# Block-sparse attention and a spatial-gating MLP: the MLP's projections interleaved, and the transposed q, k pairs split into their tiles by DMAs instead of VectorE copies

## The chip, the cores and the metric

The kernel runs on one core of one Trainium2 chip. The metric is device time in microseconds (us), lower is better. A core has five engines that run their own instruction streams and wait for one another by semaphores: TensorE (PE in the profile, with its weight loads as PEld), VectorE (DVE), ScalarE (ACT), GpSimd (POOL) and SyncE (SP), which here only issues DMAs. The DMAs are carried out by 16 DMA engines.

## The reference, cut to what matters

Attention over 4 batches of 8 heads, 768 positions, head size 64, under a block mask (blocks of 32: neighbours, first and last row and column, and three sampled blocks per row), followed by a gated MLP along the sequence:

```python
scores = scale * np.matmul(q, k.transpose(0, 1, 3, 2))        # B=4, H=8, S=768, D=64
scores = np.where(mask, scores, -1000000000.0)
attn = np.exp(scores - max) ; attn = attn / (sum + 1e-09)
x = np.matmul(attn, v)                                        # heads side by side: B, S, 512
h = np.maximum(x @ w_in, 0.0)                                 # 512 -> 1024
u, v = h[..., :512], h[..., 512:]
v_n = (v - mu) / np.sqrt(var + 1e-06)                         # over the 512 features
v_s = np.einsum('ts,bsd->btd', w_spatial, v_n) + b_spatial[None, :, None]
out = (u * v_s) @ w_out                                       # 512 -> 512
```

## The kernel before

**Staging.** Heads are handled in pairs; there are 16 pairs (p = 0 to 15), four to a batch. Loads of q, k, v (`load`, in float32, on SyncE's queue) run three pairs ahead. GpSimd casts them to bfloat16 (`prepare`: `nat_k`, `nat_q`, and `vv`). The scores need q and k with the head dimension on partitions, so each pair is transposed: for the first six pairs by TensorE (`tr_head`, `tr_pair`), for pairs 6 to 15 by a DMA transpose on SyncE (`tr_dma`), which puts both heads of the pair into one tile `tt_k` or `tt_q` of 128 partitions, the first head in partitions 0 to 63, the second in 64 to 127.

**The mask tiles.** The mask enters the scores as extra rows of the product: the tiles `qt[0..3]` and `kt[0..3]` have 64 rows of data and 24 rows that encode the block mask. Head j uses tiles j % 4. So the transposed pair must be split: rows 0 to 63 of `tt` go to rows 0 to 63 of one tile, rows 64 to 127 to rows 0 to 63 of the next. `split_pair` does that.

**The main loop** has 12 slots per pair, six per head. In a slot TensorE makes the scores of one chunk of 128 keys (`qk_exp`, two matmuls of 384 columns), ScalarE takes their exponential into `a_all`, TensorE pops some matmuls of the MLP of the batch before (from the deque `moe_q`), and multiplies one chunk of the head of seven slots earlier by its values (`av`, six matmuls; VectorE normalizes a finished head in `norm`). Slot numbers place the rest: `split_pair` of the next pair's k in slot 5 and q in slot 9, loads and `prepare` in slot 7, the DMA transposes of the pair after next (`tr_dma`) in slot 10. The program is emitted in this order and each engine runs its own part of it strictly in order, SyncE's queue included.

**The MLP** of one batch is a list of 108 matmuls of 512 columns (`moe_units`): 24 for v (six chunks of positions, four matmuls each), 24 for u, 36 for the spatial product and 24 for the output. They are spread over the 48 slots that follow slot 8 of the first pair of the next batch (52 for the third batch), about 2.25 per slot. After the four matmuls of a v chunk `v_post` takes the Relu (VectorE in the loop, ScalarE for the last batch), then the statistics on VectorE (`bn_stats`, `bn_aggr`); after every third chunk GpSimd makes the reciprocal deviations of three (`std`, `rstd`). After the four matmuls of a u chunk `u_post` takes the Relu of u on ScalarE and normalizes the v chunk of the same number (`vn`) on VectorE. The spatial product reads all six `vn`; its result becomes `gn` on VectorE and is transposed to `gt` by a DMA on SyncE, which the output matmuls read. The MLP of the last batch runs after the loop, with nothing beside it, with its gn transposed on TensorE.

**The start.** TensorE runs matmuls of zeros (`keep_warm`) between the first transposes, so that its clock rises.

Of the kernel before, what the change touches and what calls it, by code (L numbers as in the profile page):

```python
# [10 lines left out]
FP32 = mybir.dt.float32  # L11
BF16 = mybir.dt.bfloat16
I32 = mybir.dt.int32
AF = mybir.ActivationFunctionType
ALU = mybir.AluOpType
# [11 lines left out]
def kernel(  # L27
# [16 lines left out]
    nc = tc.nc  # L44

    B, H, S, D = q.shape
# [3 lines left out]
    NCH = S // 128  # L50
    HALF = S // 2
    DM = H * D
    DFF = moe_w_in.shape[1]
    DH = DFF // 2
    NDM = DM // 128
    NDH = DH // 128
    NG = H // 2
    NP = B * NG
# [5 lines left out]
    work = ctx.enter_context(tc.tile_pool(name="work", bufs=1))  # L64
# [5 lines left out]
    w_in_t = const.tile([128, NDM, DFF], BF16)  # L70
# [4 lines left out]
    mhalf = const.tile([128, NCH], FP32)  # L75

    qt = [const.tile([KR, S], BF16, name=f"qt{s}") for s in range(4)]
    kt = [const.tile([KR, S], BF16, name=f"kt{s}") for s in range(4)]
# [99 lines left out]
    def keep_warm(n, cols):  # L178
        for _ in range(n):
            nc.tensor.matmul(out=wps[:, 0:cols], lhsT=warm[:, 0:128], rhs=warm[:, 0:cols],  # L180
                             start=True, stop=True)
# [26 lines left out]
    for r in range(NR):  # L208
        nc.vector.scalar_tensor_tensor(out=allowed, in0=colidx,
                                       scalar=samp_f[:, 2 * r:2 * r + 1], in1=allowed,  # L210
                                       op0=ALU.is_equal, op1=ALU.max)
    bm = const.tile([NB, NB], BF16)
    nc.vector.tensor_scalar(out=bm, in0=allowed, scalar1=1.0, scalar2=-MASK_NEG,
                            op0=ALU.subtract, op1=ALU.mult)
# [3 lines left out]
                         func=AF.Copy)  # L218
# [6 lines left out]
    def tr_head(h, nm, copy):  # L225
        ps = psum.tile([128, S], BF16, tag="moe", bufs=2)
        for c in range(NCH):
            nc.tensor.transpose(out=ps[0:D, c * 128:(c + 1) * 128], in_=nat[nm, 0][:, c, h],  # L228
                                identity=ident)
        copy((qt if nm == "q" else kt)[h][0:D, :], ps[0:D, :])  # L230
# [15 lines left out]

    tr_head(0, "k", dve_copy)
    nc.vector.tensor_copy(out=kt[0][D:KR, :], in_=ind)
    keep_warm(2, 128)
    mq = psum.tile([128, 1024], FP32, tag="sc", bufs=2, name="mq")  # L250
    for hf in range(2):
        nc.tensor.matmul(out=mq[0:NB, hf * 512:hf * 512 + HALF], lhsT=bm,
                         rhs=ind[:, hf * HALF:(hf + 1) * HALF], start=True, stop=True)
    act_copy(qt[0][D:KR, :].rearrange("p (b c) -> p b c", b=2),
             mq[0:NB].rearrange("p (b c) -> p b c", b=2)[:, :, 0:HALF])
    tr_head(0, "q", dve_copy)
    keep_warm(6, 128)

    def mask_rows(sl):
        nc.vector.tensor_copy(out=kt[sl][D:KR, :], in_=kt[0][D:KR, :])  # L260
# [7 lines left out]
    tt = {}  # L268
# [3 lines left out]
        nc.sync.dma_start_transpose(out=tt[nm, p],  # L272
                                    in_=nat.pop((nm, p)).rearrange("p c h d -> p (c h d)"))

    def split_pair(p, nm):
        src = tt.pop((nm, p)).rearrange("x c n -> x (c n)")
        for h in range(2):
            nc.vector.tensor_copy(out=(qt if nm == "q" else kt)[(2 * p + h) % 4][0:D, :],  # L278
                                  in_=src[h * D:(h + 1) * D, :])


# [79 lines left out]
    def moe_units(b):  # L361
        last = b == B - 1
        units = []
        un = work.tile([128, NCH, DH], BF16, tag="un", bufs=2)
        vsb = work.tile([128, NCH, DH], BF16, tag="vsb", bufs=2)
        vn = work.tile([128, NCH, DH], BF16, tag="vn", bufs=2)
        gn = work.tile([128, NCH, DH], BF16, tag="gn", bufs=2)
        gt = work.tile([128, NCH, NDH, 128], BF16, tag="gt", bufs=2)
        mv = work.tile([128, NCH, 2], FP32, tag="mv", bufs=2)
        std = work.tile([128, NCH], FP32, tag="std", bufs=2)  # L370
        rstd = work.tile([128, NCH], FP32, tag="rstd", bufs=2)

        def xt(g):
            return xt_ref[b * NG + g]

        def add(n, operands, post):


            box = []

            def step(i):
                if i == 0:
                    box.append(moe_ps(last))
                lhs, rhs = operands(i)
                nc.tensor.matmul(out=box[0], lhsT=lhs, rhs=rhs,  # L385
                                 start=(i == 0), stop=(i == n - 1))
                if i == n - 1:
                    post(box[0])
            units.extend((lambda i=i: step(i)) for i in range(n))

        for tcc in range(NCH):
            def v_post(ps, tcc=tcc):
                if last:
                    nc.scalar.activation(out=vsb[:, tcc, :], in_=ps, func=AF.Relu)  # L394
                else:
                    nc.vector.tensor_scalar(out=vsb[:, tcc, :], in0=ps, scalar1=0.0,  # L396
                                            scalar2=None, op0=ALU.max)
                stats = work.tile([128, 6], FP32, tag="stats", bufs=2)
                nc.vector.bn_stats(out=stats, in_=vsb[:, tcc, :])  # L399
                nc.vector.bn_aggr(out=mv[:, tcc, :], in_=stats)  # L400
                if tcc % 3 == 2:
                    cs = slice(tcc - 2, tcc + 1)
                    nc.gpsimd.tensor_scalar(out=std[:, cs], in0=mv[:, cs, 1], scalar1=1e-6,  # L403
                                            scalar2=None, op0=ALU.add)
                    nc.gpsimd.tensor_tensor(out=rstd[:, cs], in0=std[:, cs],
                                            in1=mhalf[:, cs], op=ALU.pow)
            add(NDM, lambda g, tcc=tcc: (xt(g)[:, tcc * 128:(tcc + 1) * 128],
                                         w_in_t[:, g, DH:DFF]), v_post)

        for tcc in range(NCH):  # L410
            def u_post(ps, tcc=tcc):
                nc.scalar.activation(out=un[:, tcc, :], in_=ps, func=AF.Relu)  # L412
                nc.vector.tensor_scalar(out=vn[:, tcc, :], in0=vsb[:, tcc, :],
                                        scalar1=mv[:, tcc, 0:1],
                                        scalar2=rstd[:, tcc:tcc + 1],
                                        op0=ALU.subtract, op1=ALU.mult)
            add(NDM, lambda g, tcc=tcc: (xt(g)[:, tcc * 128:(tcc + 1) * 128],
                                         w_in_t[:, g, 0:DH]), u_post)

        def g_tr(tcc):  # L420
            ps = psum.tile([128, S], BF16, tag="moe", bufs=2, name="ps_g")
            for dhc in range(NDH):
                nc.tensor.transpose(out=ps[:, dhc * 128:(dhc + 1) * 128],  # L423
                                    in_=gn[:, tcc, dhc * 128:(dhc + 1) * 128],
                                    identity=ident)
            act_copy(gt[:, tcc].rearrange("p c n -> p (c n)"), ps[:, 0:DH])

        for tcc in range(NCH):
            def s_post(ps, tcc=tcc):
                nc.vector.scalar_tensor_tensor(out=gn[:, tcc, :], in0=ps,  # L430
                                               scalar=b_col[:, tcc:tcc + 1],
                                               in1=un[:, tcc, :], op0=ALU.add, op1=ALU.mult)
                if not last:
                    nc.sync.dma_start_transpose(out=gt[:, tcc], in_=gn[:, tcc, :])
                elif tcc > 0:
                    g_tr(tcc - 1)
            add(NCH, lambda sc, tcc=tcc: (w_spt[:, sc, tcc * 128:(tcc + 1) * 128],
                                          vn[:, sc, :]), s_post)

        for tcc in range(NCH):  # L440
            def o_post(ps, tcc=tcc):
                osb = work.tile([128, DM], FP32, tag="osb", bufs=6)
                if last and tcc == NCH - 1:
                    nc.scalar.activation(out=osb[:, 0:DM // 2], in_=ps[:, 0:DM // 2],
                                         func=AF.Copy)
                    nc.vector.tensor_copy(out=osb[:, DM // 2:DM], in_=ps[:, DM // 2:DM])
                elif tcc % 2 == 0:
                    nc.scalar.activation(out=osb, in_=ps, func=AF.Copy)
                else:
                    nc.vector.tensor_copy(out=osb, in_=ps)  # L450
                nc.sync.dma_start(
                    out=out[b].rearrange("(p c) d -> c p d", c=NCH)[tcc], in_=osb)
            if last and tcc == 1:
                units.append(lambda: g_tr(NCH - 1))
            add(NDH, lambda dhc, tcc=tcc: (gt[:, tcc, dhc, :], w_out_t[:, dhc, :]), o_post)
        return units
# [7 lines left out]
    for p in range(NP + 1):  # L464
        for s in range(12):
            g = 12 * p + s
# [15 lines left out]
            if p <= NG:  # L482
                first = 0 if p else 6
                if first <= s < first + 3:
                    tr_pair(p + 1, "k", s - first)
                elif first + 3 <= s < first + 6:
                    tr_pair(p + 1, "q", s - first - 3)
            elif p + 1 < NP and s in (5, 9):
                split_pair(p + 1, "k" if s == 5 else "q")
            if s == 10 and NG + 1 < p + 2 < NP:  # L490
                tr_dma(p + 2, "k")
                tr_dma(p + 2, "q")
# [68 lines left out]
```

The softmax here doesn't subtract the row's maximum and nothing guards it: scores larger than these inputs give would overflow.

## Time and profile before

| what | value |
|---|---|
| time, median of three runs | 224.88 us (224.37 to 226.83) |
| span of the profiled run | 224.2 us |
| TensorE busy | 214.1 us, 95% |
| VectorE busy | 128.1 us, 57% |
| ScalarE busy | 177.5 us, 79% |
| GpSimd busy | 64.4 us, 29% |
| copies that split k (`kt<-tt_k`, 20) | 9.5 us on VectorE |
| copies that split q (`qt<-tt_q`, 20) | 7.0 us on VectorE |
| statistics of v (`stats`, 24) | 16.7 us on VectorE |
| first exponential | 8.9 us after the span's start |
| last exponential | starts at 187.4 us |

Busy shares are averages over the start, the loop without an MLP (up to about 50 us), the loop with one (to about 190 us) and the tail (to the end); these have different limits. In the profile's lines a group is named by its source line, its engine, and the tiles written and read; "SPq" is SyncE's DMA queue, and the length shown there is that of issuing the transfer, not of the transfer.

### The profile page before, as it was taken

The numbers are of one execution on the slowest core, as the hardware profiler recorded it, in microseconds if no ns is written. First come the engines' busy times: TensorE is split into PE (matmuls) and PEld (weight loads), VectorE is DVE, ScalarE is ACT, GpSimd is POOL, SyncE is SP. The second block draws the span as 40 slices with busy tenths as digits, with TensorE's granted clock in tenths as the row PEclk, the third lists the DMA queues.
The fourth block names the chain that finished last, engine by engine and source line by source line (L and its number), as shares of the span: only waits on it lengthen the run. The fifth ranks groups of instructions, "written<-read, shape, count | busy, mean of one in ns | idle before, by whom it ended". The sixth has DMA issues, their size and how long they took to land.

```text
span 224.2 us, 5285 instructions
## 1 busy us (share of the span) xinstructions
PE 214.1 (95%) x2117; PEld 130.7 (58%) x2148; DVE 128.1 (57%) x282; ACT 177.5 (79%) x246; POOL 64.4 (29%) x88
## 2 busy tenths in 40 slices
PE   7999999999999999999899999999999999999993
PEld 3567777775555655665556666566556665544551
DVE  5465554556984445268983454359993433584531
ACT  5599999998789888887699888888899885266351
POOL 5435751429950701210650301210620000012000
PEclk9999999999999999999999999999999999999999
DMA  6679989996799796999756286989050224620016
GB/s 210 212 228 392 389 287 339 330 168 73 204 299 155 234 133 183 195 298 275 236 105 213 48 108 195 218 290 272 4 105 6 55 50 82 213 96 0 0 50 235
DMA packets 56093, 40.27 MB, mean 180 GB/s; under 512 B 39300, under 2 KB 51588, under 8 KB 56068
## 3 DMA queue, kind: packets, MB, share of 16 engines
q1 hardware_dynamic: 55780, 39.53, 67.3%
q10 hardware_dynamic: 288, 0.39, 0.5%
q8 instruction: 17, 0.28, 0.5%
q14 instruction: 8, 0.07, 0.1%
HBM read 24.38 MB, written 6.29 MB: 137 GB/s over the span
## 4 chain that ended last, share of the span: by engine, by line
PE 69%; DVE 14%; ACT 13%; issue 2%; DMA 2%; SPq 0%
PE ps_moe L385 24%; PE ps L289 19%; ACT a_all L293 12%; PE ps_av L305 10%; PE ps_t L385 7%; DVE vsb L396 4%; DVE stats L399 4%; PE ps_sc L385 4%; PE wps L180 2%; DVE kt L278 2%; DMA st_q<-in_q_dram 2%; DVE xn L319 2%; PE ps L228 1%; DVE mv L400 1%; PE ps_g L423 1%
## 5 line engine op out<-in xcount | busy, mean ns | idle before, releaser
L293 ACT ACTIVATE a_all<-ps 128x768 bf16<-128x768 f32 x192 | 149.9, 816 | 21.8 <-PE ps L289 13.7
L289 PE MATMUL ps<-qt,kt 88*128 88x384 bf16 x384 | 94.6, 327 | 1.3 <-DVE qt L244 0.5
L305 PEld LDWEIGHTS <-a_all 128*128 128x128 bf16 x1152 | 60.4, 97 | 39.3 <-issue 3.4
L305 PE MATMUL ps_av<-vv,a_all 128*128 128x65 bf16 x1152 | 67.8, 194 | 0.2
L385 PE MATMUL ps_moe<-w_in_t,xt 128*128 128x512 bf16 x130 | 39.6, 378 | 2.5 <-DVE vsb L396 1.8
L289 PEld LDWEIGHTS <-kt 88*128 88x128 bf16 x384 | 28.4, 98 | 4.0 <-issue 1.2
L385 PE MATMUL ps_moe<-vn,w_spt 128*128 128x512 bf16 x99 | 30.0, 378 | 0.5
L112 POOL CAST vv<-st_v 128x768 bf16<-128x768 f32 x16 | 13.5, 844 | 54.3 <-PE ps_av L305 51.1
L385 PEld LDWEIGHTS <-xt 128*128 128x128 bf16 x192 | 18.6, 97 | 16.1 <-issue 0.3
L430 DVE SCALAR_TENSOR_TENSOR gn<-ps_moe,b_col,un 128x512 bf16<-128x512 f32 x18 | 13.5, 749 | 18.9 <-PE ps_moe L385 15.6
L318 DVE RECIPROCAL rc<-ps_av 128x6 f32<-128x6 f32 x32 | 6.1, 190 | 26.1 <-PE ps_av L305 26.0
L403 POOL TENSOR_SCALAR std<-mv 128x3 f32<-128x3 f32 x8 | 2.0, 244 | 63.2 <-DVE mv L400 63.1
L385 PEld LDWEIGHTS <-w_spt 128*128 128x128 bf16 x144 | 13.7, 97 | 10.8
L385 PE MATMUL ps_moe<-w_out_t,gt 128*128 128x512 bf16 x66 | 19.1, 378 | 0.5 <-DVE gn L430 0.3
L319 DVE TENSOR_TENSOR xn<-ps_av,rc 128x384 bf16<-128x384 f32 x32 | 17.8, 558 | 1.1
L109 POOL CAST nat_k<-st_k 128x768 bf16<-128x768 f32 x15 | 12.4, 828 | 18.5 <-DMA st_k<-in_k_dram 13.9
L399 DVE BATCH_NORM_STATS2 stats<-vsb 128x6 f32<-128x512 bf16 x24 | 16.7, 694 | 1.5 <-ACT vsb L394 0.8
L396 DVE TENSOR_SCALAR vsb<-ps_moe 128x512 bf16<-128x512 f32 x18 | 12.3, 682 | 3.0 <-PE ps_moe L385 3.0
L109 POOL CAST nat_q<-st_q 128x768 bf16<-128x768 f32 x15 | 12.9, 859 | 0.0
L385 PEld LDWEIGHTS <-gt 128*128 128x128 bf16 x96 | 8.8, 97 | 6.9
L278 DVE COPY kt<-tt_k 64x768 bf16<-64x768 bf16 x20 | 9.5, 476 | 4.3 <-DMA tt_k<-nat_k 4.1
L412 ACT ACTIVATE un<-ps_moe 128x512 bf16<-128x512 f32 x18 | 11.0, 609 | 0.0
(80 smaller groups left out, 172.4 us busy)
## 6 DMA issues: line engine op xcount, KB each, us to landing
st_v<-in_v_dram SPq DMA_DIRECT2D x16, 384.0 KB, 5.5
out_dram<-osb SPq DMA_DIRECT2D x24, 256.0 KB, 2.5
st_q<-in_q_dram SPq DMA_DIRECT2D x15, 384.0 KB, 3.9
st_k<-in_k_dram SPq DMA_DIRECT2D x15, 384.0 KB, 4.9
wst<-in_moe_w_spatial_dram SPq DMA_DIRECT2D x3, 768.0 KB, 8.7
wst<-in_moe_w_in_dram SPq DMA_DIRECT2D x4, 512.0 KB, 9.2
wst<-in_moe_w_out_dram SPq DMA_DIRECT2D x2, 512.0 KB, 6.7
st_k<-in_k_dram ACTq DMA_DIRECT2D x2, 192.0 KB, 2.9
```

Source lines behind the costliest of these rows:

```text
L109: eng.tensor_copy(out=dst, in_=src)
L112: nc.gpsimd.tensor_copy(out=vv[p % 3][:, :, :, 0:D], in_=st.pop(("v", p)).rearrange("p h (c d) -> p h c d", d=D))
L278: nc.vector.tensor_copy(out=(qt if nm == "q" else kt)[(2 * p + h) % 4][0:D, :], in_=src[h * D:(h + 1) * D, :])
L289: nc.tensor.matmul(out=ps[:, hf * 512:hf * 512 + HALF], lhsT=kt[j % 4][:, ci * 128:(ci + 1) * 128], rhs=qt[j % 4][:, hf * HALF:(hf + 1) * ...
L293: nc.scalar.activation(out=a_ref[j][:, ci, :].rearrange("p (b c) -> p b c", b=2), in_=ps.rearrange("p (b c) -> p b c", b=2)[:, :, 0:HALF], ...
L305: nc.tensor.matmul(out=av_ref[j][:, qc, :], lhsT=a_ref[j][:, ci, qc * 128:(qc + 1) * 128], rhs=vv[p % 3][:, h, ci, :], start=(ci == 0), st ...
L319: nc.vector.tensor_tensor(out=xn_ref[p][:, :, h, :], in0=ps[:, :, 0:D], in1=rc.to_broadcast([128, NCH, D]), op=ALU.mult)
L385: nc.tensor.matmul(out=box[0], lhsT=lhs, rhs=rhs, start=(i == 0), stop=(i == n - 1))
L396: nc.vector.tensor_scalar(out=vsb[:, tcc, :], in0=ps, scalar1=0.0, scalar2=None, op0=ALU.max)
L399: nc.vector.bn_stats(out=stats, in_=vsb[:, tcc, :])
L412: nc.scalar.activation(out=un[:, tcc, :], in_=ps, func=AF.Relu)
L430: nc.vector.scalar_tensor_tensor(out=gn[:, tcc, :], in0=ps, scalar=b_col[:, tcc:tcc + 1], in1=un[:, tcc, :], op0=ALU.add, op1=ALU.mult)
```

## The change

It does two things, with some change at the start.

First, v and u chunks of the MLP are interleaved: v0, v1, v2, u0, v3, u1, v4, u2, v5, u3, u4, u5, where before came six v and then six u. The normalization of v chunk i moves from the u chunk i to the u chunk i + 1, the last two both to the last. This is to spread VectorE's statistics over a longer time and to give the reciprocal deviations time to come.

Second, `split_pair` issues plain DMAs from SBUF to SBUF on SyncE's queue, all four of a pair in slot 4, where VectorE made four copies in slots 5 and 9. This is to free VectorE of them. Ten pairs are split in this way, so 40 copies become 40 DMAs of 64 rows of 1536 bytes.

Third, `keep_warm` runs six more matmuls of 128 columns before the first scores.

```diff
-    keep_warm(2, 128)
+    keep_warm(4, 128)
     mq = psum.tile([128, 1024], FP32, tag="sc", bufs=2, name="mq")
...
+    keep_warm(2, 128)
     tr_head(0, "q", dve_copy)
-    keep_warm(6, 128)
+    keep_warm(8, 128)
...
-    def split_pair(p, nm):
-        src = tt.pop((nm, p)).rearrange("x c n -> x (c n)")
-        for h in range(2):
-            nc.vector.tensor_copy(out=(qt if nm == "q" else kt)[(2 * p + h) % 4][0:D, :],
+    def split_pair(p):
+        for nm in "kq":
+            src = tt.pop((nm, p)).rearrange("x c n -> x (c n)")
+            for h in range(2):
+                nc.sync.dma_start(out=(qt if nm == "q" else kt)[(2 * p + h) % 4][0:D, :],
                                   in_=src[h * D:(h + 1) * D, :])
...
-        for tcc in range(NCH):
-            def u_post(ps, tcc=tcc):
-                nc.scalar.activation(out=un[:, tcc, :], in_=ps, func=AF.Relu)
-                nc.vector.tensor_scalar(out=vn[:, tcc, :], in0=vsb[:, tcc, :],
-                                        scalar1=mv[:, tcc, 0:1],
-                                        scalar2=rstd[:, tcc:tcc + 1],
-                                        op0=ALU.subtract, op1=ALU.mult)
...
+        def u_post(tcc, ps):
+            nc.scalar.activation(out=un[:, tcc, :], in_=ps, func=AF.Relu)
+            if tcc > 0:
+                normalize(tcc - 1)
+            if tcc == NCH - 1:
+                normalize(tcc)
...
+        for i in range(NCH + 2):
+            if i < NCH:
+                in_proj(i, slice(DH, DFF), v_post)
+            if i >= 2:
+                in_proj(i - 2, slice(0, DH), u_post)
...
-            elif p + 1 < NP and s in (5, 9):
-                split_pair(p + 1, "k" if s == 5 else "q")
+            elif p + 1 < NP and s == 4:
+                split_pair(p + 1)
```

More of the change, by code (lines that the diff above doesn't have):

```diff
@@ L389, in add @@
             units.extend((lambda i=i: step(i)) for i in range(n))
-        for tcc in range(NCH):
[L392 to L408, printed above, removed]
@@ L410, in moe_units, with v_post @@
-        for tcc in range(NCH):
-            def u_post(ps, tcc=tcc):
-                nc.scalar.activation(out=un[:, tcc, :], in_=ps, func=AF.Relu)
-                nc.vector.tensor_scalar(out=vn[:, tcc, :], in0=vsb[:, tcc, :],
-                                        scalar1=mv[:, tcc, 0:1],
-                                        scalar2=rstd[:, tcc:tcc + 1],
-                                        op0=ALU.subtract, op1=ALU.mult)
-            add(NDM, lambda g, tcc=tcc: (xt(g)[:, tcc * 128:(tcc + 1) * 128],
-                                         w_in_t[:, g, 0:DH]), u_post)
+        def v_post(tcc, ps):
+            if last:
+                nc.scalar.activation(out=vsb[:, tcc, :], in_=ps, func=AF.Relu)
+            else:
+                nc.vector.tensor_scalar(out=vsb[:, tcc, :], in0=ps, scalar1=0.0,
+                                        scalar2=None, op0=ALU.max)
+            stats = work.tile([128, 6], FP32, tag="stats", bufs=2)
+            nc.vector.bn_stats(out=stats, in_=vsb[:, tcc, :])
+            nc.vector.bn_aggr(out=mv[:, tcc, :], in_=stats)
+            if tcc % 3 == 2:
+                cs = slice(tcc - 2, tcc + 1)
+                nc.gpsimd.tensor_scalar(out=std[:, cs], in0=mv[:, cs, 1], scalar1=1e-6,
+                                        scalar2=None, op0=ALU.add)
+                nc.gpsimd.tensor_tensor(out=rstd[:, cs], in0=std[:, cs],
+                                        in1=mhalf[:, cs], op=ALU.pow)
@@ new lines, in normalize @@
+        def normalize(tcc):
+            nc.vector.tensor_scalar(out=vn[:, tcc, :], in0=vsb[:, tcc, :],
+                                    scalar1=mv[:, tcc, 0:1],
+                                    scalar2=rstd[:, tcc:tcc + 1],
+                                    op0=ALU.subtract, op1=ALU.mult)
+        def u_post(tcc, ps):
[4 more added lines that the diff above has]
+                normalize(tcc)
@@ L420, in g_tr, with in_proj @@
+        def in_proj(tcc, cols, post):
+            add(NDM, lambda g: (xt(g)[:, tcc * 128:(tcc + 1) * 128], w_in_t[:, g, cols]),
+                lambda ps: post(tcc, ps))
+        for i in range(NCH + 2):
[3 more added lines that the diff above has]
+                in_proj(i - 2, slice(0, DH), u_post)
         def g_tr(tcc):
```

## The prediction

> **What bounds the kernel now.** I read the page first: TensorE is busy 95% of the span, and the chain that ended last is 69% TensorE, 14% VectorE, 13% ScalarE. An average over stages decides nothing, so I cut the span into the iterations of the outer loop (one head pair each, from the first exponential of a pair to that of the next, taken from the ScalarE timeline) and asked for busy times in each. The six that matter, with columns us of the stretch, then busy us of TensorE, weight loads, VectorE, ScalarE, GpSimd:
>
> ```profile
> 54.06:66.71 12.65, 12.06 (x122) 7.23 (x124) 12.00 (x26) 10.59 (x14) 10.00 (x11) 1.00 0.98 234
> 66.71:78.78 12.07, 11.96 (x122) 7.23 (x124) 5.40 (x14) 11.11 (x18) 5.17 (x6) 1.00 0.92 198
> ...
> 103.34:116.51 13.17, 12.11 (x123) 7.23 (x124) 12.52 (x26) 10.59 (x14) 5.74 (x9) 1.00 0.74 208
> 116.51:128.58 12.07, 11.96 (x123) 7.24 (x124) 5.36 (x14) 11.10 (x18) 3.13 (x4) 1.00 0.47 131
> ...
> 152.92:165.14 12.22, 11.68 (x121) 7.04 (x122) 11.46 (x26) 10.17 (x13) 4.58 (x7) 1.00 0.46 119
> 165.14:176.78 11.64, 11.47 (x120) 7.04 (x122) 5.21 (x15) 11.21 (x17) 0.38 (x1) 1.00 0.27 52
> ```
>
> See the pairs of lines: each holds a v stage, then the u stage after it. In the u stage TensorE is busy 11.96 of 12.07 us: that is its pace. In the v stage VectorE is busy 12.00 of 12.65 us, and the iteration is longer by 0.58, 1.10 and 0.58 us (12.65, 13.17, 12.22 less 12.07, 12.07, 11.64). That is 2.26 us, the whole of what VectorE costs in the loop. The chain in order of time agrees: in these stretches it leaves TensorE for VectorE, the k copies among its links.
>
> ```profile
> 104.23 0.71 DVE stats L399
> ...
> 108.87 0.76 DVE kt L278
> 109.65 0.89 DVE kt L278
> 110.53 0.61 DVE vsb L396
> ```
>
> Third, the timeline of the SyncE queue in the spatial stage of the second batch (start, length):
>
> ```profile
> 137.87 1.20 SPq L434 DMA_TRANSPOSE gt<-gn  x1
> 139.16 1.36 SPq L342 DMA_TRANSPOSE xt<-xn  x1
> 140.61 1.25 SPq L272 DMA_TRANSPOSE tt_k<-nat_k  x1
> 141.96 1.24 SPq L272 DMA_TRANSPOSE tt_q<-nat_q  x1
> 143.29 1.22 SPq L434 DMA_TRANSPOSE gt<-gn  x1
> 144.60 2.91 SPq L451 DMA_DIRECT2D out_dram<-osb  x4
> ```
>
> These follow one another with some 0.1 us between: from 127.06 to 152 us the queue, not what it waits for, sets when a transfer is issued. The last gt there has its gn ready at 139.51 and is issued only at 143.29.
>
> **What the Trainium skill says.** "DMA: Bandwidth & Descriptors", section "Two DMAs through the same engine are not ordered": a DMA that reads what an earlier one wrote must have its issuing engine wait for the earlier one's semaphore. So each split DMA makes SyncE wait for the tt transpose to land, with all that is queued behind it. "Perfetto Trace Analysis", section "DMA Instruction — HWDGE (DVE, Sync)": that wait is on the sequencer, and the shown length is the issue alone. The trace agrees: tt_k takes 1.2 us of queue and lands 3.8 us after issue (median). "TensorE: Matmul & The Clock Gate", Part 1: TensorE starts at half clock and is released by a free-running window of about 3.4 us of activity. Here the release came 10.4 us in (a pair of score matmuls takes 0.80 us before, 0.48 after).
>
> **Part by part.**
>
> VectorE copies removed: 20 kt at 476 ns and 20 qt at 348 ns are 16.5 us of VectorE work (groups L278), four per iteration, 1.6 us. Only the v stages feel it. Interleaving spreads the six v posts (0.68 + 0.70 + 0.18 us each) over twelve accumulations instead of six: 48 matmuls at 2.25 a slot are 21 slots of 1.0 us, with VectorE work of 9.4 (v) + 2.5 (six vn at 0.41) + 2.7 (norms) = 14.6 us. VectorE then has room, so all of the 2.26 us can come back; only v0, v1, v2 still stand back to back, and they kept pace before. Gain 2.3 us, bounds 1.9 to 2.3. The chain and the windows leave nothing else for VectorE to give: in the other iterations it is busy under 7 of 12 us.
>
> The normalization made later: in the loop hidden, since v5 is followed by 12 matmuls (5.4 us) and its chain takes about 4.5. In the tail there is nothing beside it. Before, the last v ends on TensorE at 200.75; then
>
> ```profile
> 202.58 0.30 POOL L403 TENSOR_SCALAR std<-mv 128x3 f32<-128x3 f32 x1 [1.40 <-DVE mv L400]
> 202.97 0.89 POOL L405 TENSOR_TENSOR rstd<-std,mhalf 128x3 f32<-128x3 f32 x1
> ...
> 203.89 1.06 DVE L413 TENSOR_SCALAR vn<-vsb,mv,rstd 128x512 bf16<-128x512 bf16 x3 [0.45 <-POOL rstd L405]
> ```
>
> that is, vn5 is ready 4.2 us after the last v. Before, 24 u matmuls (5.2 us at 0.216) stood in between; after, 12 (2.6 us). The spatial product starts at once and needs vn3, vn4, vn5 as its fourth to sixth operands, at 0.65, 0.86 and 1.08 us; they come at 0.95, 1.3 and 1.65. TensorE stands for about 0.6 us (0.4 to 0.9).
>
> keep_warm: six more 128-column matmuls before the first score, each 0.107 us at half clock (six take 0.75 in the chain). Two go ahead of mq, two ahead of the q transposes: 0.43 us on the path. The last two exceed the wait for the qt copy, another 0.2. Later start means about one score pair fewer at half clock, 0.15 back. Cost 0.4; if the added activity releases the clock a window earlier, the start gains about 1.2 instead.
>
> Split DMAs: 40 of 64 rows x 1536 bytes. No row of before is an SBUF to SBUF DMA. Issue: the nearest rows are plain loads and stores, 0.33 to 0.58 us; I take 0.45 plus 0.03, so four are 1.9 us of queue per iteration (1.4 to 2.4). Landing: nearest is out<-osb, 256 KB in 2.0 to 2.9 us in those stretches; I take 2.3. Engines: the 1536-byte packets of before take 68 ns, so 256 packets over 16 engines are 1.1 us per iteration, in 82 to 88 us beside a DMA share of 0.35 to 0.56. The program's order of waits shows one thing more: every issue also waits for the eighth transfer before it, and with four more per iteration that window spans less time. The longest loads land in 10 us, the queue issues about one transfer per us, so I cost this at nothing beyond the range.
>
> Does a head wait for its split? Pair 9 is first used at 102.76; its tt_q lands at 96.4, splits would be issued by about 99 to 101 and q lands by 102.3 to 103. Pair 12: 134.9, needed 140.06. Pair 14: tt_q is issued 152.7, lands 4.8 later, needed 164.56. All nearly or just in time; I take 0.3 us in all, up to 3.
>
> What the splits push back: gt. They stand in the queue after the third gt of the spatial stage (order of instructions), where the queue is full, so the last gt of batches 0 and 1 is issued up to 1.9 us later. Before, those land at 96.89 (93.6 + 3.3) and 147.14 (143.29 + 3.85); the first output matmul that reads them runs at 97.69 and 147.48: slack 0.8 and 0.34. TensorE takes its instructions in order, so it would stand 1.1 + 1.5 us if the delay is full, and 0.2 + 0.5 if the transfers, whose share is over 1.0 there, were the later limit anyway. I take 1.8. Batch 2 has no such splits, and its gt is issued at once.
>
> Sum: -2.3 + 0.6 + 0.4 + 0.3 + 1.8 = +0.8 us on 224.88: 225.7 us.
>
> **Rivals.**
>
> A, relief wins: the queue absorbs the splits (idle 106 to 113 us, and loads issued 6 us ahead of need), gt and heads in time: -2.3 + 0.6 + 0.4 = -1.3, 223.6 us; with the early clock release 222.0. For it: the windows, which show the gain plainly. Against: slack of 0.34 and 0.8 us at gt.
>
> B, the queue becomes the bound: splits wait for late tt transposes, tt of the next pair slips behind them, and the heads of pairs 9, 10, 13, 14 wait 1 us each beside full gt stalls (2.6): 0.8 + 0.8 + 4 = +5.6 less 1 shared, about 229.5 us. For it: the queue runs without pause for some 25 us in two stretches, and tt_q took 4.8 us to land at the busiest. Against: tt mostly lands 6 to 8 us ahead of use.
>
> C, nothing on the path but VectorE was: then also the tail and the warm-up cost nothing, 222.6 us. Against: the rstd link above is measured.
>
> **How the numbers follow.** Forecast 0.52; A and C together 0.26, B 0.22. Likeliest 225.7. A range of 223.0 to 228.8 takes in A at its centre, half of B, and the bounds of issue cost and stalls. 1% is 2.25 us: faster (below 222.6) only for A with the early clock or C, 0.11; slower (above 227.1) is B and the upper end of the forecast, 0.25; within, 0.64.
>
> **What would show it.** Right on VectorE: the three v iterations shrink to 12.1, 12.1 and 11.6 us, and VectorE's busy time falls by about 16 us. Right on the queue: TensorE waits for the gt DMA near 98 and 148 us, and the last gt is issued 1.5 to 2 us later against its gn. Right on the tail: TensorE or its weight loads wait for vn about 0.6 us at the start of the last spatial stage. Wrong: no wait for gt, a wait of scores for the split DMAs of more than 1 us, or a first exponential before 8.9 us.

## The result and the profile after

The changed kernel takes 235.57 us (median of four runs, 234.28 to 235.87), the kernel before beside it 225.29 us. The ratio is 1.044, 95% interval 1.037 to 1.051: slower by about 10 us. The forecast was 225.7 us with a range up to 228.8. Of the kernels below, the profiles of the DMAs from GpSimd and of those in full places were taken in slow runs (236.80 and 236.05 us), so their waits are read, but not small differences of their times.

The first page of the profile says where not to look. Its busy times (line 1, us and share of the span):

```profile
PE 216.4 (93%) x2154; PEld 130.1 (56%) x2154; DVE 115.1 (49%) x242; ACT 177.6 (76%) x246; POOL 63.5 (27%) x88
```

VectorE lost 13.0 us of work (128.1 to 115.1), TensorE is busy 2.3 us more, and the span is 9.4 us longer. So something stands and waits. The same windows as before, one for each head pair with an MLP stage beside it (p5 is the iteration of pair 5; us, then busy us of TensorE, weight loads, VectorE, ScalarE, GpSimd, then the granted clock, the DMA share and GB/s):

```profile
52.46:64.54 12.08, 12.08 (x125) 7.24 (x124) 8.21 (x18) 10.82 (x16) 7.80 (x7) 1.00 0.94 198
...
76.60:91.07 14.47, 12.23 (x125) 7.29 (x124) 4.44 (x9) 10.22 (x13) 2.37 (x3) 1.00 0.90 187
91.07:107.91 16.84, 14.26 (x131) 7.91 (x130) 5.58 (x11) 10.51 (x15) 2.43 (x3) 0.90 0.98 240
107.91:119.98 12.07, 12.07 (x125) 7.24 (x124) 8.07 (x18) 10.81 (x16) 3.45 (x5) 1.00 0.90 179
132.04:145.02 12.98, 12.23 (x125) 7.31 (x124) 4.44 (x9) 10.22 (x14) 2.43 (x3) 1.00 0.97 188
145.02:160.65 15.63, 12.62 (x130) 7.31 (x129) 5.49 (x11) 10.50 (x15) 2.43 (x3) 1.00 0.95 236
160.65:173.91 13.26, 11.79 (x123) 7.09 (x122) 8.18 (x19) 10.35 (x14) 3.45 (x5) 1.00 0.93 185
```

The lines of p8 and p12 before:

```profile
90.85:103.34 12.49, 12.32 (x128) 7.56 (x130) 6.82 (x15) 10.39 (x15) 2.09 (x3) 1.00 1.09 233
...
140.65:152.92 12.27, 12.10 (x127) 7.47 (x129) 6.81 (x15) 10.38 (x15) 2.43 (x3) 1.00 1.01 245
```

The first v stage after (p5, first line) and the second (p9, 107.91) now take 12.07 us, which is TensorE's own pace: VectorE's 0.58 and 1.10 us came back, as forecast. But p7 (14.47) and p8 (16.84), p11 (12.98) and p12 (15.63), which took 12.07, 12.49, 12.07 and 12.27 before, lost 2.4, 4.35, 0.9 and 3.35 us, and p13, which should have gained 0.58, lost 1.05. These five lose 12.1 us; p5 and p9 gain 1.7, p5 begins 1.6 us earlier (52.46 for 54.06, of which below), and the tail loses 0.6: together the 9.4 us of the spans. The view of waits of TensorE names what it stood for (total us, times, longest):

```profile
PE ps_moe L387 <- DMA gt<-gn: 5.6, 4, 2.3
PE ps L291 <- DMA qt<-tt_q: 4.5, 3, 2.2
```

Neither wait exists in the kernel before. gt are the transposes that the output matmuls read, qt the split DMAs. TensorE waits for gt in p8 (2.6 us) and p12 (3.0), and for the split q of the next pair's first head in p7 (2.2), p11 (0.75) and p13 (1.5): 10.1 of the 12.1 us that these five lose. In p8 there is 3.4 us at half clock besides (the 0.90 in its line; see the end). Both kinds of DMA are issued by SyncE, whose queue from p6 to p8 looks so (start and length of the issue, us):

```profile
72.03 1.36 SPq L280 DMA_DIRECT2D kt<-tt_k  x2
73.49 1.19 SPq L280 DMA_DIRECT2D qt<-tt_q  x2
...
77.78 1.21 SPq L446 DMA_TRANSPOSE gt<-gn  x1
...
86.99 1.17 SPq L280 DMA_DIRECT2D kt<-tt_k  x2
88.25 1.20 SPq L280 DMA_DIRECT2D qt<-tt_q  x2
89.50 1.27 SPq L446 DMA_TRANSPOSE gt<-gn  x1
...
92.52 1.20 SPq L446 DMA_TRANSPOSE gt<-gn  x1
...
99.17 1.22 SPq L446 DMA_TRANSPOSE gt<-gn  x1
```

and in the kernel before, the first and the fifth gt of the same stage:

```profile
75.96 1.20 SPq L434 DMA_TRANSPOSE gt<-gn  x1
...
87.67 1.20 SPq L434 DMA_TRANSPOSE gt<-gn  x1
```

The first gt of the stage is issued at 77.78, 4.0 us after its gn is written (73.76); before, it was 0.03 us. The fifth is issued at 92.52, 7.8 us after its gn (84.75; before 0.75), and lands at 98.43: it is the one for which TensorE stands 2.3 us. The last is issued at 99.17, 11.6 us after its gn (87.53; before 3.9), and lands at 101.64; TensorE, late already, stands only 0.3 us more for it. The q of pair 8, due in p7, is issued at 88.25 and lands at 90.36; TensorE has stood 2.2 us for it by then.

### The profile page after: what moved, and what is told of

The parts are those of the page before. It is cut to its first block, busy times and chain, and to the rows that moved or that the text cites. A ratio compares the mean times of both kernels' runs of the same rounds, so it can differ in the third digit from the quotient of the medians.

```text
span 233.6 us, 5372 instructions
## 1 busy us (share of the span) xinstructions
PE 216.4 (93%) x2154; PEld 130.1 (56%) x2154; DVE 115.1 (49%) x242; ACT 177.6 (76%) x246; POOL 63.5 (27%) x88
## 4 chain that ended last, share of the span: by engine, by line
PE 70%; ACT 13%; DMA 6%; SPq 4%; issue 2%; DVE 2%; POOL 1%; POOLq 0%; DVEq 0%
PE ps_moe L387 26%; PE ps L291 19%; ACT a_all L295 13%; PE ps_av L307 11%; PE ps_t L387 6%; DMA st_k<-in_k_dram 3%; PE ps_sc L387 3%; DMA gt<-gn 2%; PE wps L180 2%; SPq L273 1%; SPq L280 1%; SPq L446 1%; DMA qt<-tt_q 1%; PE ps L228 1%; PE ps_x L331 1%
## 5 line engine op out<-in xcount | busy, mean ns | idle before, releaser
L387 PE MATMUL ps_moe<-w_in_t,xt 128*128 128x512 bf16 x144 | 42.1, 378 | 0.0
L387 PE MATMUL ps_moe<-vn,w_spt 128*128 128x512 bf16 x108 | 31.8, 378 | 0.0
L387 PE MATMUL ps_moe<-w_out_t,gt 128*128 128x512 bf16 x72 | 22.2, 392 | 5.7 <-DMA gt<-gn 5.6
L462 DVE COPY osb<-ps_moe 128x512 f32<-128x512 f32 x9 | 6.2, 691 | 13.5 <-PE ps_moe L387 13.4
L410 DVE TENSOR_SCALAR vn<-vsb,mv,rstd 128x512 bf16<-128x512 bf16 x24 | 11.2, 488 | 2.9 <-POOL rstd L406 2.9
```

Source lines behind the costliest of these rows:

```text
L387: nc.tensor.matmul(out=box[0], lhsT=lhs, rhs=rhs, start=(i == 0), stop=(i == n - 1))
```

## The experiments

Two readings are open. The split DMAs are the loss, or the interleaving is. And if the DMAs are: the time of their issue in SyncE's queue (theory S), the standing of that queue until tt has landed (W), their bytes on the DMA engines (T), or their own latency to the head (H).

**Copies back.** `split_pair` and its call as before, all else as changed.

```diff
-            elif p + 1 < NP and s == 4:
-                split_pair(p + 1)
+            elif p + 1 < NP and s in (5, 9):
+                split_pair(p + 1, "k" if s == 5 else "q")
```

> The changed kernel with the four VectorE copies per pair back in slots 5 and 9, interleaving and six extra warm-up matmuls kept. Theory Q (the split DMAs' time in SyncE's in-order queue is the whole loss): the waits for gt and for the split heads vanish, the v iterations stay at 12.1, 12.1 and 11.6 us, the start keeps what it gained, the last spatial stage still waits 0.5 us: 225.3 - 2.3 - 1.5 + 0.6 = about 222 us. Rival I (the interleaving itself slows the spatial and output stages, by later vn and a later rstd): p8 and p12 stay over 15 us, time 230 us or more.

Measured: 223.61 us, ratio 0.994 (0.990 to 0.997); p5 to p15 take 12.07, 12.07, 12.07, 12.49, 12.07, 12.06, 12.07, 12.27, 11.64, 11.64, 10.62 us. All three v stages are at TensorE's pace, with VectorE's 16 us of copies still in place:

```profile
52.50:64.57 12.07, 11.90 (x122) 7.24 (x124) 9.71 (x22) 10.78 (x15) 7.84 (x7) 1.00 0.99 241
```

VectorE is busy 9.7 of 12.1 us here. So the interleaving alone was enough; the removal of the copies adds nothing to it. The time is 1.6 us above what was expected. 235.6 less 223.6, 12 us, is what the DMAs cost.

**The split alone**, in the kernel before.

```diff
-            nc.vector.tensor_copy(out=(qt if nm == "q" else kt)[(2 * p + h) % 4][0:D, :],
+                nc.sync.dma_start(out=(qt if nm == "q" else kt)[(2 * p + h) % 4][0:D, :],
```

> The kernel before with nothing changed but the split: four DMAs in slot 4 in place of the copies. Theory Q: the same loss in p7, p8, p11, p12 and p13 as in the changed kernel, some 12 to 13 us, less what VectorE's relief gives in the v stages (up to 1.5 us, since 1.6 us of copies per stage go): about 236 us. Rival I: under 230 us.

Measured: 233.88 us, ratio 1.036 (1.030 to 1.042). p5, p9 and p13 take 12.07, 12.07 and 12.06 us: taking the copies away relieves the first two v stages as well as interleaving does; p13 stays 0.42 us over its 11.64, 0.27 of it a wait for the split q of pair 14. p7, p8 and p12 take 14.91, 16.21 and 16.12. The loss belongs to the split, without any interleaving. That p11 loses nothing here (12.07), and that the whole is 2 us below what was expected, was not followed up.

**The warm-up alone**, in the kernel before: the three `keep_warm` lines of the change.

> The kernel before with nothing changed but the six added warm-up matmuls. If they are what released TensorE's clock at 3.9 instead of 10.4 us, the first exponential comes near 7.5 us and the time is 1.4 us lower, 223.9 us. If the release is a matter of the window's phase in that run, the first exponential comes at 9.0 to 9.4 us and the time is the same or 0.4 us higher.

Measured: 225.32 us, ratio 1.000 (0.998 to 1.002, 20 runs). In its profile the clock is released at 5.7 us and the first exponential comes at 8.24. What the other runs show of this is told at the end.

**The same DMAs from GpSimd.**

```diff
-                nc.sync.dma_start(out=(qt if nm == "q" else kt)[(2 * p + h) % 4][0:D, :],
+                nc.gpsimd.dma_start(out=(qt if nm == "q" else kt)[(2 * p + h) % 4][0:D, :],
```

> The changed kernel with the same 40 split DMAs issued by GpSimd instead of SyncE; bytes, slots and waits for the data are the same. Theory Q (the place in SyncE's queue): gt is issued within 4 us of its gn again, TensorE's wait for gt goes, time 222 to 225 us. Rival T (the added traffic on the DMA engines makes every transfer late): the waits for gt and for the split heads stay, 231 us or more. Rival H (the split is simply too slow from its landing of tt to the head's use): gt in time, but scores wait for the split at the starts of p8, p9, p13 and p14, 227 to 230 us.

Measured: 233.98 us, ratio 1.037 (1.032 to 1.042). A miss for the hope, but a clear answer. TensorE's waits and GpSimd's:

```profile
PE ps L291 <- DMA qt<-tt_q: 7.9, 4, 3.7
POOL kt L280 <- DMA tt_k<-nat_k: 36.9, 6, 9.0
```

No wait for gt is left, so with the splits out of SyncE's queue the gt come in time, beside the same traffic. But now the heads wait for their split. Issued from GpSimd these DMAs land in 2.1 to 8.4 us, median 3.5, where from SyncE it was 2.0 to 3.1, median 2.1, and GpSimd itself stands 36.9 us for tt_k (second line); p5, p6 and p9 become 16.26, 14.19 and 14.60 us, with a stretch of 6.8 us at half clock from the end of p5 into p6. Theory H holds for this queue, not for SyncE's.

**A constant source:** the DMAs read a tile that is written once, so they wait for no transpose.

```diff
-            src = tt.pop((nm, p)).rearrange("x c n -> x (c n)")
+            tt.pop((nm, p))
+            src = stand_in
```

> The changed kernel with the split DMAs reading a tile that is written once at the start, so that they wait for no transpose (the transposes still run and are not used: from pair 6 on the scores are made of constant q and k). Theory W (SyncE standing still until tt has landed is the loss): gt is issued as before, no wait for it, time 222 to 225 us. Theory S (the issue of four more transfers, 0.57 us each and 0.6 with the gaps, in a queue that is already full, is the loss): the waits for gt in p8 and p12 stay at 3 us or more each, only p13 recovers, time 230 to 233 us.

Measured: 231.71 us, ratio 1.028 (1.022 to 1.033). p7 and p8 stay at 14.39 and 16.03 us, p12 and p13 fall to 13.70 and 12.37. TensorE:

```profile
PE ps_moe L390 <- DMA gt<-gn: 4.5, 3, 2.1
PE ps L294 <- DMA qt<-stand_in: 2.7, 2, 2.2
```

In the changed kernel SyncE stands for tt_k before its splits:

```profile
SPq L280 <- DMA tt_k<-nat_k: 11.0, 4, 4.1
```

Three of these four waits, of 4.1, 2.8 and 4.1 us, end at 115.6, 127.3 and 169.9; in the first batch's stages the longest is 0.55 us. After these the constant source gains: p11, p12 and p13 together 3.7 us. p7 stays as it was to 0.1 us, and p8 gains 0.8, but without the stretch at half clock that the changed kernel has there. So the wait for tt in SyncE's queue is about a third of the loss (235.6 less 231.7, 3.9 of 12 us, by the MLPs of the second and third batch), and theory S has the rest.

**Narrow DMAs:** 64 rows of 32 bytes instead of 1536, the same count and waits.

```diff
-                nc.sync.dma_start(out=(qt if nm == "q" else kt)[(2 * p + h) % 4][0:D, :],
-                                  in_=src[h * D:(h + 1) * D, :])
+                nc.sync.dma_start(out=(qt if nm == "q" else kt)[(2 * p + h) % 4][0:D, 0:16],
+                                  in_=src[h * D:(h + 1) * D, 0:16])
```

> The changed kernel with split DMAs of 16 columns instead of 768 (64 rows of 32 bytes; the rest of each tile keeps the data of an earlier pair), with the same count, place and waits. Theory S: the issue takes as long, 0.5 us or more each, and the loss stays, 230 us or more. Rival T (bytes on the DMA engines): the loss goes with the bytes, 225 us or less.

Measured: 234.29 us, ratio 1.037 (1.032 to 1.042), with 2% of the bytes. One narrow DMA lands sooner, but its issue takes as long; the lines of the q splits in this kernel, and then in the changed one (min/median/max in ns):

```profile
L280 SPq DMA_DIRECT2D qt<-tt_q x20: 462/547/587, 55.4 to 179.6; - x20
```

```profile
L280 SPq DMA_DIRECT2D qt<-tt_q x20: 462/587/596, 55.7 to 179.9; - x20
```

Theory T falls: with hardly any bytes the time is 1.3 us lower, of 12.

**Half:** q by DMAs in slot 4, k by copies in slot 5.

```diff
+            if nm == "k":
+                nc.vector.tensor_copy(out=kt[(2 * p + h) % 4][0:D, :], in_=src[h * D:(h + 1) * D, :])
+            else:
+                nc.sync.dma_start(out=qt[(2 * p + h) % 4][0:D, :], in_=src[h * D:(h + 1) * D, :])
```

> The changed kernel with q split by DMAs in slot 4 and k by VectorE copies in slot 5: two DMAs per pair instead of four. Theory S: the queue is pushed back by 1.2 us per pair instead of 2.5, of which the slack of gt (0.3 to 0.8 us) takes a part: less than half of the loss, 225 to 229 us. If one DMA was as bad as four (theory W), 232 us or more.

Measured: 229.29 us, ratio 1.016 (1.011 to 1.020), 5.7 us over the kernel with copies: half of the loss, just over the upper edge of what was expected. No matmul waits for a gt any more (weight loads do, 2.0 us); TensorE waits for VectorE (3.9 us in total), whose k copies now stand for a tt_k that lands late (13.6 us of VectorE's time), with the vsb and osb behind them. The delay took another way to the same place.

**Where the queue is idle, where it is full.** DMAs for pairs 6, 10, 11 and 15 and copies for the rest; then DMAs for pairs 7, 8, 9, 12 and 13.

```diff
+            elif p + 1 < NP and p + 1 in (6, 10, 11, 15):      # second kernel: (7, 8, 9, 12, 13)
+                if s == 4:
+                    split_dma(p + 1)
+            elif p + 1 < NP and s in (5, 9):
+                split_pair(p + 1, "k" if s == 5 else "q")
```

> The changed kernel with DMAs splitting only pairs 6, 10, 11 and 15, whose slots fall where SyncE's queue is idle for a time; the other six pairs are split by VectorE copies in slots 5 and 9. Theory S with place (a transfer costs only where the queue is full): as the kernel with copies throughout, 223 to 225 us, no wait for gt. Rival C (each split DMA costs about the same wherever it stands, 12 us for 40): 16 of 40 cost 4.8 us, 228 us or more.

> The changed kernel with DMAs splitting only pairs 7, 8, 9, 12 and 13, those just before and in the spatial and output stages; the other five by copies. Theory S with place: nearly the whole loss, 231 to 234 us, with waits for gt in p8 and p12. Rival C: 20 of 40, half the loss, 229.5 us.

Measured: 225.52 us (ratio 1.001, 0.999 to 1.004) for the first, 235.15 us (1.038, 1.030 to 1.046) for the second. Against the kernel with copies, 16 DMAs in idle places cost 1.9 us and 20 in full places 11.5, nearly all of the 12; each is somewhat above what was expected. The 1.9 us are one stall, in p6 (14.14 us): the tt_k of pair 7, behind the DMAs of pair 6, is issued at 63.34 and lands at 71.70, where with copies throughout it was 61.53 and 66.23, and VectorE waits for it with vn queued behind; pairs 10, 11 and 15 cost nothing that is seen (p9, p10 and p14 at 12.07, 12.06 and 11.64). In full places TensorE stands for gt in p8 (2.9 us) and p12 (1.7), and no longer for split heads; in p9 and p13 it stands 1.8 and 1.9 us for VectorE, whose k copies wait for a late tt_k. So the sum is that of the changed kernel, but not each part. A price per DMA (rival C) would have given 228 and 229.5.

**From ScalarE's queue**, in slot 7.

```diff
-                nc.sync.dma_start(out=(qt if nm == "q" else kt)[(2 * p + h) % 4][0:D, :],
+                nc.scalar.dma_start(out=(qt if nm == "q" else kt)[(2 * p + h) % 4][0:D, :],
```

> The changed kernel with the split DMAs issued by ScalarE in slot 7 (by then tt has mostly landed where SyncE is not delayed). Theory S: SyncE's queue is as in the kernel before, no wait for gt. But ScalarE, busy 10.1 to 11.1 of 12.1 us with its exponentials, stands still for four issues of 0.5 us: each iteration of p5 to p14 gets up to 1 us longer, 226 to 233 us. If ScalarE's issue were free, 223.5 us.

Measured: 252.16 us, ratio 1.119 (1.112 to 1.125), far outside what was expected. p5, p11 and p12 take 17.37, 16.72 and 17.98 us. ScalarE's timeline in p5:

```profile
60.42 1.16 ACTq L280 DMA_DIRECT2D kt<-tt_k  x2
61.70 3.35 ACTq L280 DMA_DIRECT2D qt<-tt_q  x2
65.09 0.60 ACT L416 ACTIVATE un<-ps_moe 128x512 bf16<-128x512 f32 x1 [3.94 <-DMA wst<-in_moe_w_out_dram]
```

I had priced four issues at 0.5 us; here the four take from 60.42 to 65.05 us, though their tt had landed by 51.7. The last was issued at 64.56, just after the load of output weights named in the line had landed (64.48): this program's transfers use eight completion semaphores in turn, and this one's turn was that of the load eight transfers earlier. Until then ScalarE ran no exponential. That is the wait which the prediction named on SyncE and costed at nothing; on an engine with work of its own it is dear.

**The tail in its old order.** Interleaving in the loop, copies, and for the last batch six v and then six u.

```diff
-        for i in range(NCH + 2):
+        lag = NCH if last else 2
+        for i in range(NCH + lag):
             if i < NCH:
                 in_proj(i, slice(DH, DFF), v_post)
-            if i >= 2:
-                in_proj(i - 2, slice(0, DH), u_post)
+            if i >= lag:
+                in_proj(i - lag, slice(0, DH), u_post)
```

> Interleaving in the loop, VectorE copies in slots 5 and 9, and the last batch in the old order (six v, then six u). The time from the last exponential to the end goes from 37.4 back to 36.8 us, because the spatial product no longer waits for the last three vn; the loop stays as in the kernel with interleaving and copies: 0.6 us below that one, about 223.0 us. If the 0.6 us came from anything else, the tail stays at 37.4.

Measured: 222.81 us, ratio 0.990 (0.987 to 0.992, 17 runs). From the last exponential to the end it is 36.81 us, against 37.39 with the interleaved tail and 36.82 before. And the same with the warm-up as before the change:

> Interleaving in the loop, copies, the old order in the last batch, and the warm-up matmuls as in the kernel before. If the six added warm-up matmuls cost 0.4 to 0.7 us where the clock is released late and nothing where it is released early, this is 0 to 0.5 us faster than with them, within what can be measured: 222.3 to 222.8 us. It should beat both kernels by the 2.3 us of the v stages.

Measured: 222.83 us, ratio 0.988 (0.984 to 0.991). Both beat both kernels, by 1.0 to 1.2% and by over 5%; the warm-up matmuls make no difference that these runs tell.

## Why the prediction was wrong, step by step

**What bounds the kernel:** right. 2.26 us was what VectorE cost in the loop, and with interleaving and copies it all came back; in the changed kernel the part of p13 is hidden by a wait. VectorE's busy time fell by 13.0 us, not by about 16. That the two halves of the change would relieve the same 2.26 us, so that interleaving alone was enough, the prediction did not see: it costed the removed copies and the interleaving as one gain and never asked what each gives alone.

**The tail:** right, 0.6 us forecast, 0.57 measured, and shown by the kernel with the old order. The changed kernel's timeline of TensorE at the start of the last spatial product; three matmuls take 0.65 us, so TensorE stands 0.36 us before the fourth and 0.21 us within or after the next three:

```profile
214.70 0.81 PE L387 MATMUL ps_sc<-vn,w_spt 128*128 128x512 bf16 x3
215.71 1.02 PE L387 MATMUL ps_sc<-vn,w_spt 128*128 128x512 bf16 x3 [0.20 <-DVE vn L410]
```

**The start:** right in kind. Where the clock is released at 10.3 to 10.4 us, the first exponential comes at 9.58 us with the six matmuls (two kernels) and at 8.90 without (the kernel before): 0.7 us, forecast 0.4. In the profiled run of the changed kernel the release came at 3.9 us and the first exponential at 7.46. That is one of the signs named for being wrong (before 8.9 us); it was luck of that run, not a gain of the change, since with the same six matmuls the release came at 10.4 us in another kernel, and the warm-up alone makes no difference (ratio 1.000).

**What the splits push back: gt.** This is the first step that failed. The kind of mechanism was the one that the traces show: splits ahead of gt in a full queue, TensorE standing for gt. The size was not, nor which gt. The prediction pushed only the last gt of a batch back, by one pair's four splits, 1.9 us, less slack; it took 1.8 us for two batches. Measured, TensorE stood 5.6 us for gt, most of it (2.3 and 2.0) for the fifth, and in p8 the stall brought on the half clock, for which the prediction has no term (about 1.6 us, an estimate from the figures at the end). The last gt of the two batches was issued 7.7 and 5.9 us later against its gn, not 1.5 to 2. Three terms were mis-sized:

- The splits of the pair before (in p6) stand ahead of the first gt too; the prediction does not count them. Before, the queue stood idle for 2.6 us ahead of that gt. In the first batch that gt left 4.0 us late.
- Four splits take 0.57 us each and 0.1 between, 2.6 us instead of 1.9, and the tt_k transposes around them took 2.05 us of issue on average instead of 1.54. The whole queue issues for 139.5 us instead of 114.3: 25 us more, of which 22.7 are the splits.
- The delays add up from pair to pair, since the queue has no pause from p6 to p8 in which to recover: 7.7 us at the last gt of the first batch (11.6 less 3.9). The prediction computed with one iteration's worth.

**The heads' wait for their split:** the second step that failed. 0.3 us was taken, up to 3 allowed; TensorE waited 4.5 us in three places, for the first heads of pairs 8, 12 and 14; in p7 and p11 this is all of the loss but 0.3 us. This wait of more than 1 us was named as a sign of being wrong. It comes of the same queue: with a constant source, where no split waits for a tt, the 2.2 us of p7 are still there.

**The wait for the eighth transfer before**, costed at nothing, was right for SyncE: from 51 to 111 us of the changed kernel its queue never stood still for more than 0.55 us, so it was its own issues that delayed it; and with the constant source its later stands of 2.8 and 4.1 us are gone. On ScalarE's queue the same term was wrong.

**Rival B** named this outcome, stalls for gt and for heads together, and at 229.5 us undersized it for the same reason. The cause of the loss is settled by the narrow DMAs, the constant source and the pair of kernels with idle and full places: it is the time in SyncE's queue where that queue is full, about two thirds of it the issue of the splits and one third their wait for tt. Why the tt transposes take longer to issue beside the splits was not tried.

## What to carry to other kernels

A queue that only issues DMAs is an engine with a busy time: before moving work to it, add up the issue times in the stage where it runs without pause, and let the delay accumulate over all of that stage; the time of the transfer and its bytes may not matter at all. Issue costs stay with the queue while the work they replace, here copies of 0.35 to 0.48 us on an engine that was busy half of the time, would have been hidden once the MLP was interleaved. And where two edits relieve the same bound, measure each alone: one of them may be only cost.

## What the runs showed of the hardware

The wait for gt had a second price. In the 3.41 us from 96.07 TensorE was busy 1.10 us, and in the 3.42 us after it ran at half clock (the column before the last two is the granted clock):

```profile
96.07:99.48 3.41, 1.10 (x12) 0.64 (x12) 0.69 (x1) 0.73 (x3) 1.14 (x2) 1.00 1.23 157
99.48:102.90 3.42, 3.15 (x20) 1.36 (x19) 0.75 (x2) 2.11 (x3) 0.83 (x1) 0.50 0.80 233
```

The 3.15 us of work in the second stretch would have taken about half of that at full clock, so the price is some 1.6 us (an estimate).

In all fourteen traces the clock changes only at whole multiples of 3.41 us from the first release (in this one it drops after 95.57 us, which is 28 times 3.41). Cut by that grid, the loops of these traces have nine windows at full clock after which the clock was halved; TensorE was busy 0.8 to 1.5 us of 3.41 in each. In every window after which full clock went on, it was busy 1.8 us or more. So it matters where a stall falls: in the kernel with the constant source the stalls for gt in p8 are longer (3.2 against 2.6 us), but the first lies across the border of two windows, busy 2.79 and 1.88 us. The clock stayed, and p8 lost 0.8 us less.

The release of the clock at the start moves from run to run: 3.9 to 6.4 us in eleven of the profiled runs and 10.3 to 10.4 in three, with and without the added warm-up matmuls in each group, though TensorE works from 1.2 us on in all. It moves the first exponential between 7.5 and 9.6 us. The Trainium skill ("TensorE: Matmul & The Clock Gate", Part 1) has the clock released by a window of about 3.4 us that runs freely, whenever the kernel starts; the grid above agrees. In the three late runs the window that ends at 6.9 to 7.0 us did not release the clock, though TensorE is busy all through it by the profile. The same page (Part 4) says that transposes do not count as busy in the same way, and transposes of the first k fall in that window (4.7 to 5.5 us in the kernel before). But they fall in the window from 2.9 to 6.3 us of the kernel with the split alone too, and that one released it; so why the late ones are late stays open.
